# K of the first pass transposed as float32 pairs, and scores from masked two-column queries

## The chip, the cores and the metric

The kernel runs on one core of a Trainium2 chip. A core has five engines with instruction streams of their own: TensorE (PE in the profile, its weight loads PEld), VectorE (DVE), ScalarE (ACT), GpSimd (POOL) and SyncE (SP), which here only issues DMAs. The metric is the device time of one execution in microseconds, lower is better. Sixteen DMA engines move data between HBM and SBUF; matrix products are written to PSUM, eight banks of 2 KB per partition, and are copied out by ACT or VectorE.

## The reference

It is one decode step of a transformer block for two sequences, with all its gradients. Cut to what matters here:

```
B, D, H, Sk, Dh = 2, 640, 32, 4096, 128      # bf16
q = layernorm(x) @ wq                        # per head h: 128 numbers
scores = q . K[b,h,:,:] * Dh**-0.5           # 4096 numbers per (b, h)
p = softmax(scores);  o = p @ V[b,h]
h1 = x + o @ wo
out = h1 + relu(layernorm(h1) @ w1) @ w2
# and, for a given grad_out, the gradients of x, K, V, wq, wo, w1, w2
```

K and V are 64 MB each in bf16, per sequence and head one tile of 4096 x 128 (1 MB). The gradients of K and V have the same size and are outer products: the gradient of K[b,h] is a column of 4096 numbers by the row q, that of V[b,h] is p by a row.

## The kernel before, in words

There are 64 pairs (b, h). **Pass 1** runs over them, 64 iterations and two to drain. Iteration i of `p1_iter` (line 463) works on three pairs at once: it transposes K of pair i and forms its scores, takes maximum and exponential of pair i-1 and multiplies K's rows by them (line 478), and sums over V of pair i-2 (`m_part`, line 471; `u_part`, line 500). A K tile lies in SBUF as 128 partitions x 32 columns x 128 bf16: partition p holds the keys 32p to 32p+31. To form scores, each 128x128 block is transposed on PE so that the head dimension comes onto the partitions; then a matrix product with q as its moving operand gives 128 scores as one column. Eight blocks make a group: `transpose_group` (line 412) writes eight bf16 transposes to one PSUM bank, and one copy of 128x1024 bf16 brings them to SBUF (ACT, line 421; in iterations 0 to 32 the fourth group goes to VectorE, line 419). `matvec_group` (line 424) then runs eight matmuls of one column each (line 427). The transposes use two PSUM banks in turn (`banks["tps"]`), so the third group can start when the first one has been copied out.

**Pass 2** (`p2_iter`, line 837) runs over the pairs once the gradient of the attention output is known for them. It needs the products of V's rows with a gradient vector, and it does this in another form: `pair_transpose` (line 429) reads the V tile as float32, each number two neighbouring bf16 elements of the head dimension, and makes four fp32 transposes per group (line 437) in place of eight; the copy is then 128x512 fp32 (ACT, line 442). Each partition now holds the even and odd elements of two blocks, interleaved. `pair_matvec` (line 445) picks the even or the odd ones with a stride as stationary operand and multiplies by a two-column vector whose other half is zero: column 0 has the vector on partitions 0 to 63, column 1 on partitions 64 to 127, so each matmul serves both blocks, and the even and the odd product are added in PSUM (line 450). Such masked vectors are made by `pair_rows` (line 332): two matmuls with the selection matrix `sel`, and four copies of 64 partitions by VectorE; for pass 2 they lie in `gom`. Pass 2 then forms the two outer products on VectorE (line 832) and POOL issues their stores (lines 870 and 889).

The order of the work is written out by hand (`manual_schedule`): a `plan` lists which iterations of the two passes run beside each other. Pass 1 runs alone to iteration 40 (`P2_AT` is 41); from there every second iteration of pass 1 has one of pass 2 beside it, step by step; then pass 2 runs alone. Between their steps background generators (`bg`, `bg2`, `bg3`: the MLP of sequence b and its gradients in `middle_gen`, gradients of the weights in `fin_gen` and `gx_gen`) get turns at fixed rates per step. All loads stand in one list (`queue`) on SP: K of pair i, V of pair i-2, and weights at named iterations; `pump` issues the next when a buffer is free. There are 12 buffers of 1 MB (`NBIG`) at first. The last six V tiles of b = 0 are kept for pass 2 (`KEPT`), so their buffers aren't given back in iterations 28 to 33.

At the start `all_q` (line 369) multiplies five tiles of wq by x, and VectorE writes the result, for all heads and both sequences, as `qc` (line 386) and scaled as `qsc` (line 387).

Of the kernel before, what the change touches and what calls it, by code (L numbers as in the profile page):

```python
# [7 lines left out]
FP32 = mybir.dt.float32  # L8
BF16 = mybir.dt.bfloat16
# [6 lines left out]
def kernel(  # L16
# [20 lines left out]
    nc = tc.nc  # L37

    B, Sq, D = A_x.shape
    _, H, Sk, Dh = A_k_cache.shape  # L40
# [10 lines left out]
    GT = 8  # L51
# [16 lines left out]
    mats = ctx.enter_context(tc.tile_pool(name="mats", bufs=1))  # L68
# [4 lines left out]
    def pst(shape, dtype, role, name):  # L73

        k = banks[role].pop(0)
        banks[role].append(k)
        return ps.tile(shape, dtype, tag=f"bank{k}", bufs=1, name=name)
# [11 lines left out]
    def take(tag, shape, name):  # L89
        assert free[tag] > 0, (tag, name)  # L90
        free[tag] -= 1
        k = homes[tag].pop(0)
        t = pools[k].tile(shape, BF16, tag=f"big{k}", bufs=1, name=name)
        home_of[id(t)] = (tag, k, t)
        return t
# [9 lines left out]
    def give(t, to=None):  # L105
        tag, k, _ = home_of.pop(id(t))
        to = to or goes_to(tag)
        owned[tag] -= 1
        owned[to] += 1
        free[to] += 1  # L110
        homes[to].append(k)
        given_at[k] = step[0]
# [35 lines left out]
    ident_bf = const.tile([128, 128], BF16)  # L148
# [173 lines left out]
    pkp = tc.alloc_tile_pool(name="pkp", bufs=1)  # L322
    hot = pkp.tile([128, 2 * H - 1], BF16)
    nc.gpsimd.memset(hot[:], 0.0)
    nc.gpsimd.memset(hot[:, H - 1:H], 1.0)
    es = pkp.tile([128, B, H], FP32)
    qc = pkp.tile([128, H, B], BF16)
    wo_t = wop.tile([128, H, D], BF16)
    w1_t = wts.tile([128, ND, Dff], BF16)
# [2 lines left out]
    def pair_rows(dst, src, hs, bs):  # L332

        n, nb = hs.stop - hs.start, bs.stop - bs.start
        t = pst([128, 2, n, nb], FP32, "mid", "pr_ps")
        for par in range(2):
            nc.tensor.matmul(t[:, par, :, :], lhsT=sel[:, par, :, :].rearrange("p c k -> p (c k)"),
                             rhs=src[:, hs, bs], start=True, stop=True)
        for c in range(2):
            rows = slice(64 * c, 64 * c + 64)  # L340
            for par in range(2):
                nc.vector.tensor_copy(out=dst[rows, hs, bs, par, c], in_=t[rows, par, :, :])
# [26 lines left out]
    def all_q():  # L369

        zero = small.tile([128, H * B], BF16, tag="zero", bufs=1, name="zero")
        nc.vector.memset(zero[:], 0.0)
        tiles = []
        for c in range(ND):
            t = take("ld", [128, HD], "wq_t")
            nc.sync.dma_start(out=t[:], in_=wq_r[:, c, :])
            tiles.append(t)
        yield
        q_ps = pst([128, H, B], FP32, "mid", "q_ps")
        nc.tensor.matmul(q_ps[:].rearrange("p h b -> p (h b)"), lhsT=ident_bf[:], rhs=zero[:], start=True, stop=False)  # L380
        for c, t in enumerate(tiles):
            for h in range(H):
                nc.tensor.matmul(q_ps[:, h, :], lhsT=t[:, h * 128:(h + 1) * 128], rhs=x1c[:, c, :],
                                 start=False, stop=(c == ND - 1 and h == H - 1))
            give(t)
        nc.vector.tensor_copy(out=qc[:], in_=q_ps[:])
        nc.vector.tensor_scalar(out=qsc[:], in0=qc[:], scalar1=SCALE, scalar2=None, op0=ALU.mult)
        yield

# [14 lines left out]
    def warm(dst, nat, g, busy):  # L404


        for k in range(busy):
            nc.tensor.matmul(dst, lhsT=nat[:, g * GT, :],
                             rhs=nat[:, g * GT + 4 * k:g * GT + 4 * k + 4, :].rearrange("p a b -> p (a b)"),
                             start=True, stop=True)  # L410

    def transpose_group(nat, g, dve=False, busy=0):
        t_ps = pst([128, GT, 128], BF16, "tps", "t_ps")
        warm(t_ps[:].bitcast(FP32).rearrange("p a b -> p (a b)"), nat, g, busy)
        for j in range(GT):
            nc.tensor.transpose(t_ps[:, j, :], nat[:, g * GT + j, :], ident_bf[:])  # L416
        t_sb = mats.tile([128, GT, 128], BF16, tag="XT", bufs=5, name="t_sb")
        if dve:
            nc.vector.tensor_copy(out=t_sb[:], in_=t_ps[:])  # L419
        else:  # L420
            nc.scalar.copy(out=t_sb[:], in_=t_ps[:])  # L421
        return t_sb

    def matvec_group(dst, t_sb, g, vec):
        for j in range(GT):
            sc = g * GT + j
            nc.tensor.matmul(dst[:, sc:sc + 1], lhsT=t_sb[:, j, :], rhs=vec, start=True, stop=True)  # L427

    def pair_transpose(nat, g, dve=False, busy=0):


        t_ps = pst([128, GT // 2, 128], FP32, "tps", "t_ps")
        warm(t_ps[:].rearrange("p j k -> p (j k)"), nat, g, busy)
        natf = nat[:].bitcast(FP32)
        for j in range(GT // 2):
            cc = (g * GT) // 2 + j
            nc.tensor.transpose(t_ps[:, j, :], natf[:, 2 * cc:2 * cc + 2, :].rearrange("p c k -> p (c k)"), ident_f[:])  # L437
        t_sb = mats.tile([128, GT // 2, 128], FP32, tag="XT", bufs=5, name="t_sb")
        if dve:
            nc.vector.tensor_copy(out=t_sb[:], in_=t_ps[:])  # L440
        else:
            nc.scalar.copy(out=t_sb[:], in_=t_ps[:])  # L442
        return t_sb

    def pair_matvec(dst, t_sb, g, vecs):
        v = t_sb[:].bitcast(BF16).rearrange("p j (k two) -> p j k two", two=2)
        for j in range(GT // 2):
            sc = g * GT + 2 * j
            for par in range(2):
                nc.tensor.matmul(dst[:, sc:sc + 2], lhsT=v[:, j, :, par], rhs=vecs[:, par, :],  # L450
                                 start=(par == 0), stop=(par == 1))
# [11 lines left out]
    def p1_iter(i, dve_group, busy):  # L463

        c = S1[i] if i < NP1 else None
        p = S1[i - 1] if 1 <= i <= NP1 else None
# [36 lines left out]

        if c is not None:
            b, h = pairs[i]
            q = qc[:, h, b:b + 1]
            c["KT0"] = transpose_group(c["K"], 0, busy=busy)
            c["KT1"] = transpose_group(c["K"], 1)
        yield
        if r is not None:  # L510
            r["m"] = pst([128, 132], FP32, "m", "m_ps")
# [17 lines left out]
            p["pk"] = []  # L529
            pk_tile(0)  # L530
        if c is not None:
            c["KT2"] = transpose_group(c["K"], 2, busy=busy)
            c["bank"] = pst([128, 512], FP32, "sps", "s_ps")
            c["s"] = c["bank"][:, 0:NSC]
            matvec_group(c["s"], c.pop("KT0"), 0, q)
        yield
        if r is not None:
            m_part(2)
        if p is not None:
            pk_half(0)  # L540
        if c is not None:
            matvec_group(c["s"], c.pop("KT1"), 1, q)
            c["KT3"] = transpose_group(c["K"], 3, dve_group)
        yield
        if r is not None:
            u_part()
            m_part(3)
        if c is not None:
            matvec_group(c["s"], c.pop("KT2"), 2, q)
        if r is not None:  # L550
            m_part(4)
        if p is not None and hp % OG == OG - 1:
# [15 lines left out]
        if r is not None:  # L568
            m_part(7)
        if c is not None:  # L570
            matvec_group(c["s"], c.pop("KT3"), 3, q)
            rmax = small.tile([128, 1], BF16, tag="rmax", name="rmax")
            nc.vector.reduce_max(out=rmax[:], in_=c["s"], axis=AX.X)
            c["rmax"] = rmax
# [522 lines left out]
    def pump():  # L1097
        while queue:
# [11 lines left out]
            queue.pop(0)  # L1110

    first_q = all_q()
    next(first_q)
    pump()
# [15 lines left out]
    for n, (i, j) in enumerate(plan):  # L1130
# [56 lines left out]
        for k, _ in enumerate(p1_iter(i, i < H + 1, 0)):  # L1187
            for _ in range(at.get(k, 0)):
                if g2 is not None:
                    p2_step()  # L1190
            if k == 5:
                a_heads(i)
            pump()

            spread[0] = 1 if i < P2_AT else 2
            at_k[0] = k
            if i >= P2_AT:
                slot[0] = int(k == 6 or (k == 1 and j is None))
            elif i > H + 1:
                slot[0] = {1: 2, 3: 1, 4: 1, 6: 1}.get(k, 0)  # L1200
            else:
                slot[0] = int(k in (1, 6))
            bg_step(0, rate)
            bg_step(1, 0.0)
# [43 lines left out]
```

## Time and profile before

| | |
|---|---|
| three runs | 911.12, 912.86, 912.86 us; median 912.86 |
| span of the profiled execution, first to last instruction | 908.6 us, 4.3 under the median |
| PE / PEld busy | 740.8 (82%) / 620.3 (68%) us |
| DVE busy | 692.1 us (76%) |
| ACT busy | 530.7 us (58%) |
| POOL busy | 173.1 us (19%) |
| moved by DMA | 363.00 MB, mean 400 GB/s |
| mean granted TensorE clock | 0.791 |

The profile is one execution. "Busy" is time with an instruction of that engine in flight; matmuls overlap and their ends are modelled, so starts are the surer marks. A line of the timeline gives start and length in us, engine, line of the code, operation, what is written and read, and how many in a row; "[0.19 <-ACT ...]" is idle time before it and what ended that. A line of a group gives count, busy time in us and mean length in ns, then the idle time of the engine ahead of it. The chain of waits is followed back from the last instruction, at each step to what released it; what is not on it cost nothing by itself. "L421" is line 421 of the kernel.

### The profile page before, as it was taken

The page shows a single profiled execution, that of the slowest core. Times are in us where ns is not written, and L with a number is a line of the kernel's source. Part 1 is how long each engine was busy: PE and PEld are TensorE (multiplying, and loading weights), DVE is VectorE, ACT ScalarE, POOL GpSimd, SP SyncE. Part 2 cuts the span into 40 slices and gives each one's busy share as a digit, 9 for nine tenths or more (in the row PEclk, how much of TensorE's full clock was granted, in tenths as well). Part 3 has the DMA queues.
Part 4 walks back from the last instruction along what each step waited for, and adds up shares of the span by engine and source line. Part 5 has one row for each costly group of instructions (what it writes and reads, how often), then busy time and mean ns, then how long its engine had stood idle before and what let it go on. Part 6 is the DMA issues. An engine that isn't in the chain of part 4 may idle for free.

```text
span 908.6 us, 26495 instructions
## 1 busy us (share of the span) xinstructions
PE 740.8 (82%) x11227; PEld 620.3 (68%) x11227; DVE 692.1 (76%) x1282; ACT 530.7 (58%) x1096; POOL 173.1 (19%) x329
## 2 busy tenths in 40 slices
PE   3899999999989898997866844886799778949780
PEld 3788888888878787887765844665667566735560
DVE  2565787877879787786879697986798459899982
ACT  1666665567777777675743443654577656537650
POOL 1232223323201111010011111121222111111120
PEclk9999999999999999898997585655557555555655
DMA  9999999999889999999999999999999999999996
GB/s 364 420 409 404 408 399 409 418 419 362 308 296 339 421 420 423 422 422 420 417 388 406 412 425 413 402 400 392 397 400 389 424 425 425 423 427 425 425 422 261
DMA packets 56262, 363.00 MB, mean 400 GB/s; under 512 B 5680, under 2 KB 11696, under 8 KB 15312
## 3 DMA queue, kind: packets, MB, share of 16 engines
q1 hardware_dynamic: 34704, 212.18, 57.9%
q0 software_dynamic: 18432, 134.23, 35.6%
q10 hardware_dynamic: 3008, 14.91, 4.1%
q8 instruction: 88, 1.44, 0.6%
q14 instruction: 30, 0.25, 0.1%
HBM read 212.16 MB, written 149.13 MB: 398 GB/s over the span
## 4 chain that ended last, share of the span: by engine, by line
PE 36%; DMA 27%; DVE 18%; ACT 9%; issue 7%; POOL 0%; SPq 0%; POOLq 0%; ACTq 0%; DVEq 0%
DMA out_dram<-gK 11%; DMA Vt<-in_A_v_cache_dram 10%; PE m_ps L471 9%; PE t_ps L416 8%; PE t_ps L437 6%; DVE gV L832 5%; ACT t_sb L421 4%; DVE gK L832 4%; PE s_ps L427 4%; DVE junk L658 3%; PE u_ps L500 3%; DMA wqs<-in_A_wq_dram 3%; DMA out_dram<-gV 2%; DVE pk L478 2%; DMA Kt<-in_A_k_cache_dram 2%
## 5 line engine op out<-in xcount | busy, mean ns | idle before, releaser
L421 ACT COPY t_sb<-t_ps 128x1024 bf16<-128x1024 bf16 x223 | 217.8, 1018 | 45.6 <-PE t_ps L416 45.3
L442 ACT COPY t_sb<-t_ps 128x512 f32<-128x512 f32 x256 | 149.8, 588 | 132.0 <-PE t_ps L437 128.9
L478 DVE TENSOR_TENSOR pk<-Kt,ep 128x2048 bf16<-128x2048 bf16 x128 | 156.3, 1221 | 57.9 <-ACT ep L526 29.1
L437 PE MATMUL t_ps<-ident_f,Wt 128*128 128x128 f32 x848 | 190.9, 371 | 1.0 <-ACT t_sb L421 1.0
L471 PE MATMUL m_ps<-pk,Vt 128*128 128x129 bf16 x2048 | 171.3, 222 | 11.7 <-DMA Vt<-in_A_v_cache_dram 10.3
L832 DVE TENSOR_TENSOR gK<-rb,gsp 128x2048 bf16<-128x2048 bf16 x128 | 152.5, 1225 | 22.2 <-DMA out_dram<-gV 20.4
L832 DVE TENSOR_TENSOR gV<-rb,pp 128x2048 bf16<-128x2048 bf16 x128 | 153.0, 1219 | 20.9 <-DMA out_dram<-gK 18.0
L416 PE MATMUL t_ps<-ident_bf,Kt 128*128 128x128 bf16 x2048 | 152.3, 223 | 8.2 <-DMA Kt<-in_A_k_cache_dram 2.3
L437 PEld LDWEIGHTS t_ps<-ident_f,Wt 128*128 128x128 f32 x848 | 131.4, 191 | 32.4 <-issue 26.1
L471 PEld LDWEIGHTS <-Vt 128*128 128x128 bf16 x2048 | 125.0, 99 | 41.4 <-issue 30.0
L416 PEld LDWEIGHTS <-Kt 128*128 128x128 bf16 x2048 | 125.2, 100 | 16.3 <-issue 10.4
L450 PEld LDWEIGHTS <-t_sb 128*128 128x128 bf16 x2048 | 95.7, 106 | 44.4 <-issue 18.8
L450 PE MATMUL dp_ps<-gom,t_sb 128*128 128x2 bf16 x2048 | 95.1, 167 | 9.2 <-ACT t_sb L442 8.0
L488 POOL COPY pk<-ep 128x16 bf16<-128x16 bf16 x80 | 64.9, 812 | 188.2 <-ACT ep L526 159.9
L427 PE MATMUL s_ps<-qc,t_sb 128*128 128x1 bf16 x2048 | 88.1, 164 | 1.6 <-DVE t_sb L419 0.8
L889 POOL DMA_DIRECT2D out_dram<-gV x64 | 34.3, 536 | 277.0 <-DVE gV L832 198.3
L870 POOL DMA_DIRECT2D out_dram<-gK x64 | 34.1, 533 | 253.6 <-DVE gK L832 196.5
L427 PEld LDWEIGHTS <-t_sb 128*128 128x128 bf16 x2048 | 77.5, 97 | 4.4 <-ACT t_sb L421 1.2
L942 ACT CAST ot<-o_ps 128x512 bf16<-128x512 f32 (+4 forms) x160 | 70.3, 489 | 13.7 <-DMA out_dram<-ot 9.3
L859 ACT ACTIVATE rb<-dp_ps,rt 128x256 bf16<-128x256 f32 x64 | 30.4, 476 | 59.8 <-PE dp_ps L854 58.5
L585 ACT CAST MT<-m_ps 128x128 bf16<-128x128 f32 x64 | 17.1, 268 | 72.8 <-PE m_ps L471 72.7
L658 DVE CUSTOM_DVE_ANT_0 junk<-wo_t,hbc 128x640 bf16<-128x640 bf16 x64 | 52.4, 818 | 0.2
(197 smaller groups left out, 781.0 us busy)
## 6 DMA issues: line engine op xcount, KB each, us to landing
Kt<-in_A_k_cache_dram SPq DMA_DIRECT2D x64, 1024.0 KB, 16.0
Vt<-in_A_v_cache_dram SPq DMA_DIRECT2D x64, 1024.0 KB, 15.5
out_dram<-gV POOLq DMA_DIRECT2D x64, 1024.0 KB, 15.4
out_dram<-gK POOLq DMA_DIRECT2D x64, 1024.0 KB, 15.3
Wt<-in_A_v_cache_dram SPq DMA_DIRECT2D x53, 1024.0 KB, 14.0
wq_t<-in_A_wq_dram SPq DMA_DIRECT2D x5, 1024.0 KB, 8.9
wo_t<-in_A_wo_dram SPq DMA_DIRECT2D x4, 1280.0 KB, 18.7
wqs<-in_A_wq_dram SPq DMA_DIRECT2D x5, 1024.0 KB, 17.2
```

The lines of the kernel that those rows point to most:

```text
L416: nc.tensor.transpose(t_ps[:, j, :], nat[:, g * GT + j, :], ident_bf[:])
L421: nc.scalar.copy(out=t_sb[:], in_=t_ps[:])
L427: nc.tensor.matmul(dst[:, sc:sc + 1], lhsT=t_sb[:, j, :], rhs=vec, start=True, stop=True)
L437: nc.tensor.transpose(t_ps[:, j, :], natf[:, 2 * cc:2 * cc + 2, :].rearrange("p c k -> p (c k)"), ident_f[:])
L442: nc.scalar.copy(out=t_sb[:], in_=t_ps[:])
L450: nc.tensor.matmul(dst[:, sc:sc + 2], lhsT=v[:, j, :, par], rhs=vecs[:, par, :], start=(par == 0), stop=(par == 1))
L471: nc.tensor.matmul(r["m"][:, 0:129], lhsT=r["V"][:, sc, :], rhs=r["pk"][sc // HALF][:, sc % HALF, 0:129], start=(sc == 0), stop=(sc == NSC ...
L478: nc.vector.tensor_tensor(out=p["pk"][k][:, :, 0:128].rearrange("p s (a two) -> p s a two", two=2), in0=p["K"][:, sl, :].rearrange("p s (a ...
L488: nc.gpsimd.tensor_copy(out=col, in_=e)
L658: nc.vector.tensor_tensor_reduce(out=junk[0:kc, 0:width], in0=in0, in1=in1, scale=1.0, scalar=0.0, op0=ALU.mult, op1=ALU.add, accum_out=acc)
L832: nc.vector.tensor_tensor(out=pairs_view(dst[:, sl, :]), in0=row.rearrange("p (a two) -> p a two", two=2)[:, None, :, :].to_broadcast([128 ...
L942: nc.scalar.copy(out=ot[0:P, k, n0:n0 + nn], in_=o_ps[0:P, 0:nn])
```

## The change

Pass 1 now uses pass 2's two helpers for K. `transpose_group` and `matvec_group` are gone. A masked form of all queries, `qm`, is made once at the start: one memset by POOL, then `pair_rows` over all 32 heads and both sequences. The number of copies, their order and the engine of each stay as they were, and so does the number of score matmuls (32 per tile); there are 16 transposes per K tile in place of 32. The loads, their order and the buffers are unchanged, and the SBUF buffers and the PSUM banks of the transposes keep their number and bytes.

```diff
@@ -324,6 +324,8 @@
     es = pkp.tile([128, B, H], FP32)
+    qm = pkp.tile([128, H, B, 2, 2], BF16)
+    nc.gpsimd.memset(qm[:], 0.0)
     qc = pkp.tile([128, H, B], BF16)
@@ -384,6 +386,7 @@
         nc.vector.tensor_copy(out=qc[:], in_=q_ps[:])
+        pair_rows(qm, qc, slice(0, H), slice(0, B))
         nc.vector.tensor_scalar(out=qsc[:], in0=qc[:], scalar1=SCALE, scalar2=None, op0=ALU.mult)
@@ -409,23 +412,6 @@
-    def transpose_group(nat, g, dve=False, busy=0):
-        t_ps = pst([128, GT, 128], BF16, "tps", "t_ps")
-        warm(t_ps[:].bitcast(FP32).rearrange("p a b -> p (a b)"), nat, g, busy)
-        for j in range(GT):
-            nc.tensor.transpose(t_ps[:, j, :], nat[:, g * GT + j, :], ident_bf[:])
-        t_sb = mats.tile([128, GT, 128], BF16, tag="XT", bufs=5, name="t_sb")
...
-    def matvec_group(dst, t_sb, g, vec):
-        for j in range(GT):
-            sc = g * GT + j
-            nc.tensor.matmul(dst[:, sc:sc + 1], lhsT=t_sb[:, j, :], rhs=vec, start=True, stop=True)
-
@@ -503,9 +489,9 @@
-            q = qc[:, h, b:b + 1]
-            c["KT0"] = transpose_group(c["K"], 0, busy=busy)
-            c["KT1"] = transpose_group(c["K"], 1)
+            q = qm[:, h, b, :, :]
+            c["KT0"] = pair_transpose(c["K"], 0, busy=busy)
+            c["KT1"] = pair_transpose(c["K"], 1)
@@ -529,24 +515,24 @@
-            c["KT2"] = transpose_group(c["K"], 2, busy=busy)
+            c["KT2"] = pair_transpose(c["K"], 2, busy=busy)
             c["bank"] = pst([128, 512], FP32, "sps", "s_ps")
             c["s"] = c["bank"][:, 0:NSC]
-            matvec_group(c["s"], c.pop("KT0"), 0, q)
+            pair_matvec(c["s"], c.pop("KT0"), 0, q)
...
-            matvec_group(c["s"], c.pop("KT1"), 1, q)
-            c["KT3"] = transpose_group(c["K"], 3, dve_group)
+            pair_matvec(c["s"], c.pop("KT1"), 1, q)
+            c["KT3"] = pair_transpose(c["K"], 3, dve_group)
...
-            matvec_group(c["s"], c.pop("KT2"), 2, q)
+            pair_matvec(c["s"], c.pop("KT2"), 2, q)
...
-            matvec_group(c["s"], c.pop("KT3"), 3, q)
+            pair_matvec(c["s"], c.pop("KT3"), 3, q)
```

More of the change, by code (lines that the diff above doesn't have):

```diff
@@ L410, in warm @@
                              start=True, stop=True)
-    def transpose_group(nat, g, dve=False, busy=0):
-        t_ps = pst([128, GT, 128], BF16, "tps", "t_ps")
-        warm(t_ps[:].bitcast(FP32).rearrange("p a b -> p (a b)"), nat, g, busy)
-        for j in range(GT):
-            nc.tensor.transpose(t_ps[:, j, :], nat[:, g * GT + j, :], ident_bf[:])
-        t_sb = mats.tile([128, GT, 128], BF16, tag="XT", bufs=5, name="t_sb")
[L418 to L422, printed above, removed]
-    def matvec_group(dst, t_sb, g, vec):
-        for j in range(GT):
-            sc = g * GT + j
-            nc.tensor.matmul(dst[:, sc:sc + 1], lhsT=t_sb[:, j, :], rhs=vec, start=True, stop=True)
     def pair_transpose(nat, g, dve=False, busy=0):
```

## The prediction

> **What bounds the kernel now.** I read the 40 slices of the page first. The row "DMA" says when the DMA engines are full, "GB/s" what they then move, "PEclk" the clock that TensorE was granted.
>
> ```profile
> PEclk9999999999999999898997585655557555555655
> DMA  9999999999889999999999999999999999999996
> GB/s 364 420 409 404 408 399 409 418 419 362 308 296 339 421 420 423 422 422 420 417 388 406 412 425 413 402 400 392 397 400 389 424 425 425 423 427 425 425 422 261
> ```
>
> A slice is 22.7 us. The DMA engines are full nearly everywhere; the hole is in slices 9 to 12, at 205 to 295 us. 363 MB at the 420 GB/s of the full slices take 864 us of the span's 908.6; the difference is the hole, the two ends and slower mixtures of packets. A change that takes work from engines can gain only where the DMA engines are not full. The windows give the same by stage (columns: length, busy time of PE, PEld, DVE, ACT and POOL with instructions, granted clock, DMA share, GB/s).
>
> ```profile
> 20.20:190.00 169.80, 161.39 (x3139) 141.31 (x3140) 119.14 (x224) 102.78 (x203) 49.13 (x84) 0.99 1.02 410
> 190.00:230.00 40.00, 39.30 (x826) 34.71 (x823) 26.93 (x64) 25.78 (x51) 13.61 (x21) 1.00 0.97 383
> 230.00:257.00 27.00, 24.12 (x471) 21.00 (x469) 23.58 (x62) 20.46 (x38) 6.13 (x12) 1.00 0.80 308
> 257.00:296.00 39.00, 35.45 (x671) 31.23 (x668) 31.56 (x77) 30.05 (x61) 4.75 (x9) 1.00 0.87 316
> 296.00:455.00 159.00, 141.69 (x2566) 125.65 (x2567) 124.16 (x249) 112.97 (x234) 16.98 (x28) 0.94 1.01 421
> ```
>
> Against 420 GB/s the three middle rows lack 40 x 37/420 = 3.5, 27 x 112/420 = 7.2 and 39 x 104/420 = 9.7 us, together 20.4 us. That is the ceiling of the change. The reason of the hole stands in the code and in SP's issues: the last six V tiles of batch row 0 are kept for pass 2, so 6 of the 12 buffers drop out in iterations 28 to 33, and from 188 us SP issues one tile each 5 to 6 us, waiting for VectorE's release of K. From there the pace of the compute sets when tiles are loaded.
>
> So what paces an iteration of pass 1? PE's timeline of one (start, length, line; ends are modelled, so I read from start to start):
>
> ```profile
> 122.43 1.05 PE L416 MATMUL t_ps<-ident_bf,Kt 128*128 128x128 bf16 x16
> ...
> 123.38 0.63 PE L471 MATMUL m_ps<-pk,Vt 128*128 128x129 bf16 x8
> 124.14 0.61 PE L416 MATMUL t_ps<-ident_bf,Kt 128*128 128x128 bf16 x8
> ...
> 127.95 1.05 PE L416 MATMUL t_ps<-ident_bf,Kt 128*128 128x128 bf16 x16
> ```
>
> An iteration is 127.95 - 122.43 = 5.52 us. Eight m_ps matmuls take 0.47 (0.94 for 16 at 126.81 in the same answer), so PE is free at 123.85 and starts the third transpose group only at 124.14. It waits 0.29 us for its PSUM bank, one of two, until ACT has copied the first group out. Smaller waits: 0.1 at 125.71 and 0.03 at 125.03. So PE works about 5.10 us and is held up 0.42 us by the copies. The chain of waits says the same: it passes through "ACT t_sb L421", 1.02 us, in nearly each iteration from 37 to 226 us.
>
> On this the Trainium skill ("Trainium Kernel Development and Optimization", Performance Expectations) has a rule: matmul busy time is a bad measure because matmuls are pipelined, and weight-load time is better. PE's 39.3 of 40 us would leave this change nothing at all; PEld's 34.7 leaves 13%, and the starts above, which decide, leave 8%.
>
> **The change part by part.** *Copies out of PSUM* (two groups of the page):
>
> ```profile
> L421 ACT COPY t_sb<-t_ps 128x1024 bf16<-128x1024 bf16 x223 | 217.8, 1018 | 45.6 <-PE t_ps L416 45.3
> L442 ACT COPY t_sb<-t_ps 128x512 f32<-128x512 f32 x256 | 149.8, 588 | 132.0 <-PE t_ps L437 128.9
> ```
>
> The K copies take the second form, which pass 2 has already: 1018 - 588 = 430 ns less each, 223 x 0.43 = 96 us of ACT in all, four (three where VectorE takes one) per iteration. The first copy then ends 0.43 us earlier than the bank is waited for: the 0.29 us goes, and most of the small waits. What is late next is PE itself, at 5.10 us.
>
> *Transposes.* 64 tiles x 16 in fp32 in place of 64 x 32 in bf16. Both stand at full clock in one stretch of the mixed stage:
>
> ```profile
> 302.72 0.60 PE L437 MATMUL t_ps<-ident_f,Vt 128*128 128x128 f32 x4
> 303.16 0.34 PE L450 MATMUL dp_ps<-gom,t_sb 128*128 128x2 bf16 x8
> 303.36 0.86 PE L471 MATMUL m_ps<-pk,Vt 128*128 128x129 bf16 x12
> ...
> 313.28 0.61 PE L416 MATMUL t_ps<-ident_bf,Kt 128*128 128x128 bf16 x8
> 313.73 0.34 PE L427 MATMUL s_ps<-qc,t_sb 128*128 128x1 bf16 x8
> 313.93 0.40 PE L471 MATMUL m_ps<-pk,Vt 128*128 128x129 bf16 x4
> ```
>
> Four fp32 transposes take 303.16 - 302.72 = 0.44 us, eight bf16 ones 0.45. So halving their number saves PE nothing: twice the time each. Other fp32 groups there are at 0.44 to 0.49. Eight fp32 ones in a row at full clock, as K's first two groups will be, are not in the trace; if their weight loads (141 ns) were not hidden, a group would be 4 x 0.141 = 0.56, or +0.44 us per iteration. Bounds 0 to +0.44; I take 0, by the groups of four.
>
> *Scores.* Eight matmuls per group before and after. The masked two-column form is pass 2's L450: 303.36 - 303.16 = 0.20 us, against 313.93 - 313.73 = 0.20. Nothing.
>
> *VectorE's copy* of the fourth group (33 iterations): 684 ns now; the fp32 form on VectorE isn't in the trace. Its fp32 reads of PSUM, 287 ns for 128 elements (L519) and 188 for 32 (L573), extend to 287 + 384 x 1.03 = 683 ns; ACT's 588 is the other end. Between 0 and -0.1 us, I take 0.
>
> *Start.* qm adds one memset on POOL, two matmuls and four casts of 64x64, about 4 x 0.23 us (the row of L386) behind the cast of qc that ends at 18.94 us. Queued behind them are qsc, not needed until pass 2, and VectorE's first copy at 24.2 us. Ready at about 20.3 us; the first score is at 23.1 us. Hidden behind the first K tile (lands 20.1 us) and its copies; without that cover, 1.4 us once. SP's list of loads, POOL's and ACT's stores are not moved in order.
>
> *By stage.* 20 to 190 us: full DMA engines at 410 GB/s, nothing (upper bound: 418 GB/s as in the later slices would give 170 x 8/418 = 3.3 us). 190 to 230: seven iterations (30 to 36) x 0.42 = 2.9 us, and part of a lead: the landing records put V of iteration 29 at 197.1, used at 200.0, and K of iteration 33 at 204.7, used at 210.75. A faster compute reaches 190 us with that lead used up; I take 1.5 of the 2.9 us. Together 4.4 (bound 6.0, K's lead). 230 to 257: the chain lies on VectorE.
>
> ```profile
> 246.34 1.14 DVE pk L478
> 247.48 0.67 DVE junk L658
> 248.23 0.67 issue
> 248.97 1.14 DVE pk L478
> ```
>
> (Columns: start, length, what; "junk L658" are the background's products, and "issue" here is another of them.) VectorE's work is not changed: 0 (bounds 0 to 5 x 0.42 = 2.1). 257 to 296: the chain holds five pieces of "ACT t_sb L421" (1.02, 0.41, 0.87, 0.86, 0.86); at about 0.4 each 2.0 us (bounds 0 and 22 copies x 0.43 = 9.5). From 296 us the DMA engines are full, and pass 2's instructions are unchanged; what was won stays as a shift. Sum: 4.4 + 2.0 = 6.4 us off the profiled execution, 908.6 to 902.2 us of span. The three runs have the median 912.86, 4.3 us above the span; I carry that over: 912.86 - 6.4 = **906.5 us**.
>
> **Rivals.** *A: hidden, within 0.2%* (1.8 us; about what a measurement of this kernel can tell from no change). For it: the DMA engines are full in most of the span, and what is won at 230 us may only be waited away at 287.8 us, where the chain holds 8.8 us of a V load and PE stands 1.6 us. Then 0.5 to 1.5 us remain: about 911.8. Against it: that load is issued when a buffer comes free, so it moves with the compute.
>
> *B: slower, through the clock.* PE now waits for DMA in lumps in place of small stalls, and its granted clock falls. The row for 296 to 455 us, where PE waits for V tiles, is granted 0.94, slice by slice down to 0.82; at 20 to 190 us it is 0.99. An iteration of 5.10 us at full clock becomes worse than 5.52 once the mean clock is under 5.10/5.52 = 0.92. At 0.91, the mean of the five slices from 341 to 454 us, it is 5.60: 0.08 x 36 iterations = 2.9 us, about 915.8; in full half clock windows up to twice that. Against it: waits of up to 1.4 us at 142 and 166 us left the clock at 1.00. The skill's rule ("TensorE: Matmul & The Clock Gate", Part 1) is that an idle window of about 3.4 us halves the clock; PE's longest wait for a tile between 21 and 296 us is 1.6 us, so by the rule alone B would not come and the sum would stay.
>
> *C: more than the sum.* ACT is also the feeder in 230 to 296 us; if VectorE's order there is itself held up by late exponentials, the bounds add up: 6.0 + 2.1 + 4 = 12 us, 900.8.
>
> *D: fp32 transposes at 0.56 us per group* take back 0.44 of 0.42 us: 912 to 914, with A in its effect.
>
> **How the numbers follow.** Forecast (902 to 910 us) 0.52, C 0.14, A and D 0.21, B 0.13. Faster by over 0.2%: 0.66; within: 0.21; slower: 0.13. The range leaves out the ends of C and of B: 899 to 915.5.
>
> **What would show it.** Right: K copies on ACT at about 590 ns; starts of iterations 5.1 us apart where no tile is waited for; GB/s in slices 9 to 12 higher; the start of pass 2's unmixed part (455 us) earlier by about 6. Groups of four fp32 transposes at 0.44 us from start to start, also in pairs. Wrong: those at 0.56; a clock under 0.95 before 205 us; or faster iterations with the hole as deep as before, only longer waits for V.

## The result, and the profile after

| | before | changed |
|---|---|---|
| median of 12 runs | 912.86 us (910.53 to 915.5) | 909.6 us (906.59 to 913.86) |
| ratio | | 0.9966, 95% interval 0.9951 to 0.9982 |
| span of the profiled execution | 908.6 us | 905.5 us |

Faster by 0.34%, 3.1 us by the ratio (1.6 to 4.5). The forecast was 6.4: the right way, inside the range, and twice the size. A second comparison (section 8 below) gave 0.9946 (0.9926 to 0.9966), 4.9 us.

The slices of the page of the changed kernel, as before:

```profile
PEclk9999999999999899999885776655555555555655
DMA  8999999999879999999999999999999999999997
GB/s 361 420 409 403 409 398 410 420 417 388 335 306 377 377 406 425 421 424 421 411 398 392 411 423 394 423 398 396 407 401 388 426 420 423 419 423 416 419 421 296
```

The hole in slices 9 to 12 is shallower (362, 308, 296, 339 became 388, 335, 306, 377), but slice 13 has fallen from 421 to 377 and slice 14 from 420 to 406. The stages (columns as before: length, PE, PEld, DVE, ACT, POOL busy, granted clock, DMA share, GB/s):

```profile
20.20:190.00 169.80, 158.03 (x2689) 138.42 (x2689) 122.91 (x227) 69.21 (x206) 67.09 (x85) 1.00 1.02 410
190.00:230.00 40.00, 40.00 (x739) 35.83 (x738) 28.10 (x70) 17.95 (x53) 15.45 (x22) 1.00 0.99 399
230.00:257.00 27.00, 25.07 (x429) 21.26 (x427) 25.04 (x65) 14.74 (x39) 6.70 (x13) 1.00 0.85 324
257.00:296.00 39.00, 34.63 (x569) 30.86 (x565) 31.73 (x74) 21.38 (x60) 4.97 (x9) 0.96 0.91 349
296.00:340.00 44.00, 42.19 (x689) 36.45 (x687) 36.47 (x75) 25.26 (x70) 5.64 (x9) 0.96 0.98 390
```

I turn these into time by bytes: a stage that moves more GB/s than the first profile of before has won (difference x length / 420) us. 190 to 230: 16 x 40/420 = 1.5; 230 to 257: 16 x 27/420 = 1.0; 257 to 296: 33 x 39/420 = 3.1. At 296 us the changed kernel is 5.6 us ahead, not far from the 6.4. From 296 to 340 us it moves 390 where before moved 422, and loses 32 x 44/420 = 3.4 us of it. Up to 190 us nothing changed: 410 and 410. PE's starts agree: its 45th matmul s_ps<-neg_ident,rmax (one per pair) starts at 294.80 us before and at 289.44 in the changed kernel, 5.4 us earlier; the last, the 64th, at 457.56 and 455.04, 2.5 us earlier. The prediction had named "earlier by about 6" there as a sign of being right.

Two groups of the page (count, busy us, mean ns, idle ahead) show the new copies and K's transposes:

```profile
L428 ACT COPY t_sb<-t_ps 128x512 f32<-128x512 f32 x479 | 274.4, 586 | 214.6 <-PE t_ps L423 208.9
L423 PE MATMUL t_ps<-ident_f,Kt 128*128 128x128 f32 x1024 | 155.1, 284 | 6.6 <-DMA Kt<-in_A_k_cache_dram 6.3
```

All of ACT's copies of transposes are at 586 ns now. An iteration of pass 1 on PE (start, length, line):

```profile
50.39 1.07 PE L423 MATMUL t_ps<-ident_f,Kt 128*128 128x128 f32 x8
51.30 0.22 PE L503 MATMUL s_ps<-neg_ident,rmax 128*128 128x128 bf16 x1
51.35 0.63 PE L457 MATMUL m_ps<-pk,Vt 128*128 128x129 bf16 x8
51.83 0.60 PE L423 MATMUL t_ps<-ident_f,Kt 128*128 128x128 f32 x4
52.27 0.34 PE L436 MATMUL s_ps<-qm,t_sb 128*128 128x2 bf16 x8
...
52.90 0.63 PE L423 MATMUL t_ps<-ident_f,Kt 128*128 128x128 f32 x4
53.47 0.62 PE L486 MATMUL u_ps<-pk,hot 128*32 128x512 bf16 x8
...
55.60 1.07 PE L423 MATMUL t_ps<-ident_f,Kt 128*128 128x128 f32 x8
```

The third group now follows m_ps at once (51.35 + 0.47 = 51.82): the 0.29 us of waiting is gone. But the iteration is 55.60 - 50.39 = 5.21 us, not 5.10. From the fourth group to u_ps it still takes 53.47 - 52.90 = 0.57 us for four transposes that take 0.44 elsewhere.

Why slice 13 fell stands in windows of 2 us of the changed kernel:

```profile
288.00:290.00 2.00, 1.12 (x9) 0.93 (x9) 1.99 (x5) 0.94 (x4) 0.00 (x0) 1.00 0.99 315
290.00:292.00 2.00, 0.00 (x0) 0.00 (x0) 0.00 (x0) 0.28 (x1) 0.00 (x0) 1.00 1.01 418
292.00:294.00 2.00, 1.61 (x21) 1.54 (x22) 1.09 (x2) 0.38 (x1) 0.00 (x0) 0.71 1.01 422
294.00:296.00 2.00, 2.00 (x28) 1.94 (x26) 2.00 (x3) 1.53 (x6) 0.15 (x1) 0.50 1.02 426
296.00:298.00 2.00, 2.00 (x21) 1.94 (x18) 0.78 (x2) 0.76 (x3) 0.38 (x1) 0.50 0.99 418
298.00:300.00 2.00, 2.00 (x30) 1.15 (x28) 0.31 (x1) 0.56 (x1) 0.00 (x0) 0.58 1.03 434
300.00:302.00 2.00, 2.00 (x40) 1.98 (x39) 1.26 (x3) 0.74 (x2) 0.00 (x0) 1.00 0.63 238
```

PE, now earlier, stands 2.4 us (to 292.0) for the V tile that was issued at 282.1. Then it is granted half its clock for 6.8 us: four fp32 transposes take 0.85 us from start to start (293.38 to 294.23) where they take 0.44 at full clock. SP waits 10.8 us for VectorE's release of a K tile before it issues the next V tile at 300.94, and at 300 us the DMA engines run dry (share 0.63). Before, PE stood 1.6 us at this place and kept its clock. The same load in the chain of waits (start, length), changed kernel first:

```profile
282.08 9.89 DMA Vt<-in_A_v_cache_dram
287.79 8.79 DMA Vt<-in_A_v_cache_dram
```

It is issued 5.7 us earlier, but takes 1.1 us longer and so lands 4.6 us earlier: 0.8 of PE's 5.4 us of lead are waited away here, ahead of the half clock.

### The profile page after: what moved, and what is told of

Read it like the earlier page. It is cut to its first block, busy times and chain, and to the rows that moved or that the text cites. A ratio compares the mean times of both kernels' runs of the same rounds, so it can differ in the third digit from the quotient of the medians.

```text
span 905.5 us, 24516 instructions
## 1 busy us (share of the span) xinstructions
PE 742.8 (82%) x10205; PEld 620.3 (68%) x10205; DVE 696.1 (77%) x1286; ACT 444.7 (49%) x1096; POOL 192.4 (21%) x330
## 4 chain that ended last, share of the span: by engine, by line
PE 42%; DMA 25%; DVE 18%; issue 6%; ACT 6%; SPq 1%; POOL 0%; POOLq 0%; ACTq 0%; DVEq 0%
PE t_ps L423 18%; DMA Vt<-in_A_v_cache_dram 13%; PE m_ps L457 9%; DVE gV L818 5%; DMA out_dram<-gV 4%; DVE gK L818 4%; DMA out_dram<-gK 3%; PE s_ps L436 3%; ACT t_sb L428 3%; DMA wqs<-in_A_wq_dram 3%; DVE gxj L644 2%; PE u_ps L486 2%; PE o_ps L922 2%; PE dp_ps L436 2%; DVE pk L464 2%
## 5 line engine op out<-in xcount | busy, mean ns | idle before, releaser
L428 ACT COPY t_sb<-t_ps 128x512 f32<-128x512 f32 x479 | 274.4, 586 | 214.6 <-PE t_ps L423 208.9
L436 PEld LDWEIGHTS <-t_sb 128*128 128x128 bf16 x4096 | 179.0, 102 | 47.0 <-issue 18.8
L423 PE MATMUL t_ps<-ident_f,Wt 128*128 128x128 f32 x848 | 196.5, 379 | 0.2 <-ACT t_sb L428 0.2
L423 PE MATMUL t_ps<-ident_f,Kt 128*128 128x128 f32 x1024 | 155.1, 284 | 6.6 <-DMA Kt<-in_A_k_cache_dram 6.3
L423 PEld LDWEIGHTS t_ps<-ident_f,Wt 128*128 128x128 f32 x848 | 135.7, 196 | 35.1 <-issue 29.3
L423 PEld LDWEIGHTS t_ps<-ident_f,Kt 128*128 128x128 f32 x1024 | 112.6, 144 | 10.9 <-PE s_ps L436 4.6
L474 POOL COPY pk<-ep 128x16 bf16<-128x16 bf16 x80 | 83.2, 1042 | 163.6 <-ACT ep L512 87.8
L436 PE MATMUL s_ps<-qm,t_sb 128*128 128x2 bf16 x2048 | 87.4, 164 | 1.5 <-DVE t_sb L426 1.5
L644 DVE CUSTOM_DVE_ANT_0 gxj<-wqs,gqr 128x1024 bf16<-128x1024 bf16 x40 | 48.8, 1221 | 2.4 <-DMA wqs<-in_A_wq_dram 2.2
L831 DVE SCALAR_TENSOR_TENSOR gsp<-dp_ps,negdot,P_bf 128x64 bf16<-128x64 f32 x64 | 18.0, 281 | 42.3 <-PE dp_ps L436 42.0
```

Source lines behind the costliest of these rows:

```text
L474: nc.gpsimd.tensor_copy(out=col, in_=e)
L644: nc.vector.tensor_tensor_reduce(out=junk[0:kc, 0:width], in0=in0, in1=in1, scale=1.0, scalar=0.0, op0=ALU.mult, op1=ALU.add, accum_out=acc)
```

## The experiments

Theory **copy**: the gain comes from the shorter copies on ACT alone, in the hole alone. Rivals: it comes from fewer transposes (**PE**), or the time saved up to 190 us is carried on (**lead**). Theory **clock**: half clock takes back part of what was won; rival **DMA**: the full DMA engines take it back anyway. Ratios are to runs of before on the same chip.

**1. The copies alone** (e1_copy_view), on the kernel before:

```diff
-            nc.vector.tensor_copy(out=t_sb[:], in_=t_ps[:])
+            nc.vector.tensor_copy(out=t_sb[:].bitcast(FP32), in_=t_ps[:].bitcast(FP32))
         else:
-            nc.scalar.copy(out=t_sb[:], in_=t_ps[:])
+            nc.scalar.copy(out=t_sb[:].bitcast(FP32), in_=t_ps[:].bitcast(FP32))
```

> The kernel before, its bf16 transposes and one-column scores kept; only the copies of the transposed K out of PSUM go through a float32 view (128x512 float32 in place of 128x1024 bf16). Theory 'copy' (all that the change wins comes from the shorter copies on ACT; fp32 transposes and two-column scores are neutral on PE): copies at about 590 ns, iterations 5.2 us apart at 50 us, time as the changed kernel, ratio to before 0.995 to 0.998. Rival 'PE' (it comes from halving the number of transposes): iterations at 5.5 us, ratio 1.000.

Ratio 0.9974 (0.9955 to 0.9994); again on another chip (e9_view_again):

> The float32 view of the copies alone, a second time. Theory 'copy': ratio as the changed kernel's two results, 0.9946 to 0.9966, or a little below, since its iterations came 0.04 us closer (5.17 against 5.21). Rival: the fp32 transposes with masked queries are worth something of their own beside the copies; then this stays above them, at 0.9974 or more.

0.9929 (0.9902 to 0.9956). ACT's copies of K take 586 ns in the first. Its PE timeline:

```profile
51.28 1.05 PE L416 MATMUL t_ps<-ident_bf,Kt 128*128 128x128 bf16 x16
...
52.69 0.61 PE L416 MATMUL t_ps<-ident_bf,Kt 128*128 128x128 bf16 x8
53.14 0.34 PE L427 MATMUL s_ps<-qc,t_sb 128*128 128x1 bf16 x8
...
56.45 1.05 PE L416 MATMUL t_ps<-ident_bf,Kt 128*128 128x128 bf16 x16
```

5.17 us per iteration with the old transposes and the old queries. Two edited lines give what the change gives; "PE" falls. Which of the two is faster the ratios don't tell: 0.9974 and 0.9929 against 0.9966 and 0.9946, with overlapping intervals.

**2. The change without shorter copies** (e2_wide_copy): pass 1's copies of the changed kernel through a bf16 view of both tiles.

```diff
+        src, dst = (t_ps[:].bitcast(BF16), t_sb[:].bitcast(BF16)) if wide else (t_ps[:], t_sb[:])
...
-            nc.scalar.copy(out=t_sb[:], in_=t_ps[:])
+            nc.scalar.copy(out=dst, in_=src)
```

> The changed kernel, its fp32 transposes and masked queries kept; only the copies of K go through a bf16 view again (128x1024 bf16). Theory 'copy': copies at about 1018 ns, iterations 5.5 us apart again, ratio to before 1.000 (0.999 to 1.002). Rival 'PE': iterations stay at 5.2 us and the ratio at 0.9966.

Ratio 1.0043 (1.0025 to 1.0062): slower than before, which neither theory had. The copies take 1016 ns. PE's timeline:

```profile
53.96 1.07 PE L423 MATMUL t_ps<-ident_f,Kt 128*128 128x128 f32 x8
...
54.92 0.63 PE L458 MATMUL m_ps<-pk,Vt 128*128 128x129 bf16 x8
55.70 0.65 PE L423 MATMUL t_ps<-ident_f,Kt 128*128 128x128 f32 x4
56.19 0.34 PE L437 MATMUL s_ps<-qm,t_sb 128*128 128x2 bf16 x8
...
59.53 1.07 PE L423 MATMUL t_ps<-ident_f,Kt 128*128 128x128 f32 x8
```

The wait is back (54.92 + 0.47 to 55.70), and the iteration is 5.57 us, 0.05 over before's 5.52, as the changed kernel is 0.04 over the view alone. So the fp32 transposes and masked queries are not a gain on PE but a small cost: eight fp32 ones in a row take 0.91 us (53.96 to 54.87), sixteen bf16 ones 0.89. Over the 15 iterations of the hole that is 0.75 us, less than the 3.9 us of the ratio. By bytes its profiled execution loses 1.3 us up to 296 us (377, 302 and 312 GB/s in the three stages) and 2.3 more from 296 to 340 us (400 GB/s), where its granted clock is 0.96. One execution doesn't tell whether the others lose it there too, so the rest of this loss stays open.

**3. to 5. The change in a part of the iterations** (e3_until30, e4_30to45, e5_from46), both forms in one kernel:

```diff
+            new = 30 <= i < 46        # the others: i < 30, i >= 46
+            tg, mv = (pair_transpose, pair_matvec) if new else (transpose_group, matvec_group)
+            q = qm[:, h, b, :, :] if new else qc[:, h, b:b + 1]
```

> Both forms in one kernel: the changed form (fp32 pair transposes, masked queries) in iterations 0 to 29 of pass 1, the form before in the others. Theory 'hole' (the change wins only where the DMA engines are not full, 205 to 296 us): iterations at 50 us are 5.2 us apart, but the tiles then come too late, GB/s from 230 to 296 us as before, ratio 1.000 (0.998 to 1.001). Rival 'lead' (what is saved while the DMA engines are full is carried into the hole): 1.5 to 2 us at 230 us, ratio 0.998.

> The changed form in iterations 30 to 45 alone (about 195 to 300 us), the form before in the others. Theory 'hole': all of the gain is here, GB/s from 190 to 296 us as in the changed kernel (399, 324, 349), ratio 0.9966 (0.995 to 0.998). Rival 'lead': some 1.5 us less, ratio 0.998 to 0.999.

> The changed form in iterations 46 to 63 alone (from 305 us on, beside pass 2), the form before in the others. Both theories: the DMA engines are full there, ratio 1.000 (0.999 to 1.002), GB/s from 296 to 455 us 421 as before. A gain there would mean that ACT, which is freed of 0.43 us per copy, also paces the mixed stage.

| iterations with the new form | ratio |
|---|---|
| 0 to 29 | 1.0004 (0.9988 to 1.0021) |
| 30 to 45 | 0.9970 (0.9950 to 0.9990) |
| 46 to 63 | 0.9995 (0.9976 to 1.0013) |
| all (e8_after_again, same chip) | 0.9946 (0.9926 to 0.9966) |

Two windows each, of the first, the second and the third:

```profile
230.00:257.00 27.00, 24.68 (x462) 21.70 (x460) 23.38 (x62) 20.44 (x37) 6.61 (x12) 0.95 0.78 297
257.00:296.00 39.00, 35.72 (x673) 31.50 (x672) 31.65 (x78) 29.75 (x61) 4.74 (x9) 1.00 0.85 317
```

```profile
230.00:257.00 27.00, 25.08 (x407) 21.79 (x406) 22.98 (x58) 14.55 (x39) 6.93 (x12) 0.96 0.80 301
257.00:296.00 39.00, 35.30 (x595) 30.84 (x593) 32.04 (x79) 21.62 (x60) 5.72 (x9) 1.00 0.91 342
```

```profile
230.00:257.00 27.00, 25.11 (x462) 22.13 (x462) 23.11 (x60) 20.02 (x37) 6.59 (x12) 0.94 0.79 301
257.00:296.00 39.00, 35.72 (x673) 31.49 (x672) 31.65 (x78) 29.74 (x61) 4.74 (x9) 1.00 0.85 313
```

Only the second fills the hole: 342 GB/s at 257 to 296 us against 317 and 313 (before: 316). In the windows from 230 to 257 us all three were granted 0.94 to 0.96 of the clock, so that e4's 301 GB/s stays under the 324 that was expected. Thirty faster iterations while the DMA engines are full (5.21 us at 50 us in e3), and eighteen more beside pass 2, each gain nothing that can be measured. "Hole" holds: e3's interval leaves out the 0.998 of "lead". e4's does not, it holds the forecasts of both; the 0.0024 between e4 and the whole change is within their intervals.

**6. and 7. Work for PE while it would stand** (e6_fill45, e7_fill4), on the changed kernel:

```diff
         if r is not None:
+            for _ in range(32 if i in (45,) else 0):        # e7: (45, 53, 57, 61)
+                nc.tensor.matmul(r["m"][:, 0:128], lhsT=ident_bf[:], rhs=ident_bf[:], start=True, stop=True)
             m_part(0)
```

> The changed kernel with 32 matmuls of 128 columns more in iteration 45, ahead of the sum over V that waits for its tile at 290 us (PE stands 2.4 us there in the changed kernel, and is then granted half its clock from 293 to 300 us). The output is the same. Theory 'clock' (that half clock takes 2.5 to 3 of the 5.7 us back that were won by then): the clock stays at 1.00 to 340 us, the sums over V from the 45th tile on start 2.5 us earlier than in the changed kernel, and the time is 907 us, ratio to before 0.994. Rival 'DMA' (what is won is waited away before 455 us, since the DMA engines are full there): the clock stays, the starts at 306 us are earlier, those at 440 us are not, ratio 0.9966 as the changed kernel.

> As the run before it, with the 32 matmuls in iterations 45, 53, 57 and 61, where PE stands over 2 us for a V tile and the clock falls to half after it. Output the same. Theory 'clock': no half clock from 23 to 455 us, ratio 0.991 to 0.994 (each avoided drop of 6.8 us is worth up to 3 us). Rival 'DMA': ratio 0.9966 again, with the waits for V longer by what PE is faster.

Ratios 0.9955 (0.9932 to 0.9977) and 0.9966 (0.9941 to 0.9991): no gain over the change that could be told from none. The profile of e6 says little: that execution, at 912.7 us its second slowest, was granted half clock at 111, 166 and 230 us already. That of e7 has the clock at 1.00 there:

```profile
296.00:340.00 44.00, 41.64 (x713) 36.28 (x710) 38.23 (x78) 25.86 (x72) 5.46 (x9) 1.00 1.01 422
340.00:455.00 115.00, 102.99 (x1664) 90.60 (x1661) 83.84 (x172) 57.29 (x157) 11.18 (x19) 0.93 1.00 413
```

It moves 422 GB/s from 296 to 340 us and keeps the 4.6 us it had won (398, 316 and 345 GB/s in the three stages), but from 340 to 455 us it moves 413 against 421, which is 8 x 115/420 = 2.2 us lost. In that stretch it was granted half clock from 373 to 383 us and from 445 to 452 us in spite of the added matmuls, 0.93 on the mean as in the changed kernel without them. So the condition of "clock" was not met, and e7 doesn't decide between the two, though its ratio is the one that "DMA" had. That the clock stays at 1.00 near 293 us isn't shown to come from the added matmuls either: the next run keeps it there without them. "Clock" explains the 3.4 us of one execution; as an explanation of the median it isn't shown.

**8. The change again** (e8_after_again), which gave the 0.9946 above:

> The changed kernel again, on the same chip as the three before it. Ratio 0.9966 (0.995 to 0.998). For theory 'clock': if the half clock at 293 us belongs to the schedule and not to one execution, this profile shows it again between 288 and 305 us, with GB/s from 296 to 340 us under 405; if it depends on where the wait falls, it may be missing, and then the lead of 5 to 6 us at 296 us is kept to 455 us.

```profile
288.00:290.00 2.00, 2.00 (x38) 2.00 (x35) 2.00 (x4) 0.59 (x4) 1.20 (x2) 1.00 1.02 381
290.00:292.00 2.00, 0.60 (x5) 0.23 (x3) 1.45 (x5) 1.04 (x2) 0.00 (x0) 1.00 0.99 320
292.00:294.00 2.00, 1.58 (x24) 1.51 (x25) 1.06 (x2) 0.45 (x1) 0.00 (x0) 1.00 1.02 430
```

The wait at 291 us is 1.25 us this time and the clock stays at 1.00. By bytes this execution won 0.5, 0.7 and 2.7 us in the three stages (388, 319, 345 GB/s), 3.9 in all, and kept it (423 GB/s from 296 to 340 us; by PE's starts 4.2 us at the 45th and 4.6 at the 64th s_ps<-neg_ident,rmax). The drop at 293 us belongs to one execution.

**9. The kernel before again** (e11_before_look):

> The kernel before once more, for its granted clock from 190 to 340 us. If the half clock after a wait depends on the execution and not on the change, some executions of this kernel show it there too, with GB/s from 190 to 340 us below those of its first profile (383, 308, 316, 422). If the change brings it, the clock is 1.00 in this stretch again.

```profile
230.00:257.00 27.00, 25.32 (x467) 22.38 (x466) 22.83 (x60) 19.85 (x36) 6.62 (x12) 0.94 0.76 296
```

Half clock from 230.1 to 233.5 us: a granted 0.94, and 296 GB/s where its first profile had 308, so 0.8 us lost. Both kernels meet such drops, in some executions, and the first profile of before was one without any from 34 to 361 us. It was also one of the shorter ones: here the time is 911.2 us for a span of 909.4, so the span of 908.6 belongs to some 910.4 us, and not to the median of 912.86. Two executions of the same kernel also end pass 1 at different times: the 64th s_ps<-neg_ident,rmax starts at 457.56 us in the first and at 459.95 us in this one.

**10. Where the last 0.1 us stands** (e10_u_after_m), on the changed kernel:

```diff
+            m_part(3)
             u_part()
-            m_part(3)
```

> The changed kernel with the sums u_ps put behind the fourth part of m_ps in place of ahead of it; output the same. On the 0.1 us per iteration that the prediction put down to ACT's copies and that stayed: if it belongs to the start of u_ps (its 32-column weights), the stretch from the fourth transpose group to what follows falls from 0.57 to 0.45 us, the same 0.1 us stands between m_ps and u_ps, and iterations stay at 5.2 us. If it belongs to the copies or to the transposes, it stays behind the transposes.

```profile
54.14 0.64 PE L423 MATMUL t_ps<-ident_f,Kt 128*128 128x128 f32 x4
54.61 0.40 PE L457 MATMUL m_ps<-pk,Vt 128*128 128x129 bf16 x4
54.94 0.62 PE L486 MATMUL u_ps<-pk,hot 128*32 128x512 bf16 x8
```

The transposes now take 0.47 us to the next start, and the four m_ps before u_ps 0.33 in place of 0.24. The 0.1 us goes with u_ps, so it was no wait for a copy of K. Whether it comes from the 32-column weights isn't shown. (One run; 906.1 us.)

## Why the prediction was right or wrong, point by point

- **The ceiling: only the hole can pay.** Right: e3, e4 and e5 show it from three sides.
- **Copies, 430 ns less each.** Right: 586 against 1018.
- **Transposes and scores cost PE the same.** Nearly: 0.91 against 0.89 us for the pair of groups and 0.20 against 0.20 for the scores; 0.04 to 0.05 us per iteration more (e1 against the change, e2 against before). Rival D, 0.56 us per group, fell.
- **VectorE's copy, 0 to -0.1 us.** Right: 684 ns before and after.
- **An iteration at 5.10 us.** Wrong in size: 5.21. Of 0.42 us put down to the copies 0.31 went. 0.1 belonged to the start of u_ps (e10). It stood in the timeline as a late start, and I gave it to ACT without a line that named ACT.
- **190 to 230 us, 4.4.** This is the term that was mis-sized most, and in both executions: 1.5 us by bytes in the profiled one, 0.5 in the second (by PE's starts at 231 us 2.8 and 1.3). The 1.5 us of lead in it was not found as a gain: with the new form up to iteration 29 alone the ratio was 1.0004. And seven iterations at 0.31 are 2.2, not 2.9.
- **230 to 257 us, nothing, since VectorE paces.** Wrong in the other direction, 1.0 and 0.7 us. The lines that the prediction shows are from 246 us on; the chain of the same window also holds two copies of K, which at 0.43 less each would be 0.9 us:

```profile
231.64 0.81 ACT t_sb L421
232.96 0.90 ACT t_sb L421
```

- **257 to 296 us, 2.0.** Too low: 3.1 and 2.7 us.
- **Sum at 296 us.** 5.6 and 3.9 us against 6.4 (the view alone, e1 and e9: 5.2 and 5.3, from 390, 330, 350 and 393, 328, 349 GB/s). In the profiled execution the sum is nearly right because errors of opposite sign cancel, which is luck.
- **"What was won stays as a shift."** This is the step that failed in the profiled execution: 3.4 us were lost between 296 and 340 us. The mechanism is rival B's, a lump of waiting and then half clock, at a place where I had excluded it because PE's longest wait there was 1.6 us before. That wait became 2.4 us, since PE was earlier and the tile, though issued earlier, took 9.9 us to land in place of 8.8. Rival A named the same V load. In the second execution the shift stayed.
- **The 4.3 us carried over from the span.** About 2 us of it are outside the span in every run (907.52 against 905.5 in the changed kernel); the rest is that the profiled execution of before was shorter than the median one, without half clock from 34 to 361 us. The forecast of the difference doesn't use it.
- **The median.** 3.1 and 4.9 us by the two ratios, with intervals from 1.6 to 6.8. The smaller sum at 296 us explains 1 to 2 us of what is missing. How much of the rest is half clock on average, how much is waiting in the full stages after 340 us, stays open: the ratios of e6 and e7 can't be told from the change's.

In short, the mechanism of the copies and of the hole was right. What failed is the size of the term for 190 to 230 us (4.4 in the sum, 1.5 and 0.5 measured) and, in the profiled execution, the shift that was to stay (3.4 us of it were lost).

## What to carry to other kernels

Where the DMA engines were full, thirty faster iterations were worth nothing (ratio 1.0004); count a gain only in the stretch where they are not, and compare bytes moved by stage to see where it comes and where it goes. A copy that only moves bits can be made through a wider type: two edited lines did here what a new transpose and masked queries did. Don't count a late start on PE as a wait for another engine unless a line names that engine. And read the chain of a whole stage, not a part of it, before a term is set to nothing.

## What the runs showed of the hardware that was not expected

- ACT's copy out of PSUM follows the number of elements, not of bytes: the same 2 KB per partition take 1018 ns as 1024 bf16 and 586 ns as 512 fp32. VectorE's copy takes 684 ns in both forms.
- Half clock came after short waits: in the second execution of the changed kernel at 111.8 us, after waits of 1.03 and 1.28 us that lay close together. In four executions (e4, e5, e6 and e11) it came between 228.6 and 230.5 us with no wait of PE over 0.2 us in the 4 us before; in e11 at 230.1 us, after 70 matmuls hf_ps of one column each among others from 227.2 to 230.1 us. The same 70 left the clock at 1.00 in the first profile of before, at nearly the same time (227.2 to 230.1 us), so they alone don't decide it; what does isn't shown. The Trainium skill ("TensorE: Matmul & The Clock Gate", Part 1) speaks of an idle window of about 3.4 us; here the drops that ended before 455 us last 3.4, 6.8 or 10.2 us, whole windows of that length, but PE need not be idle for one.
